# Sequence 0 of an attention-pack kernel with a channel mix: k and v loaded in runs of six tokens, p in one transfer, a planner without lag on one engine, and two tiles at a time in block 1's gates

## The chip, the cores and the metric

One NeuronCore of a Trainium2 chip runs the whole program. The time is the device time of one execution in microseconds. An execution that was also profiled gives the trace; its span runs from its first to its last instruction.

## The reference

Eight sequences (B) of 576 tokens (S), 8 heads (H) of 64 (D). For each sequence and head, 32 packed queries p attend to k and v, and the 576 queries q attend to the 32 packed results. The heads' outputs stand side by side as x (576 tokens by 512), which goes through a channel mix.

```
def sm_attn(qq, kk, vv):
    s = scale * np.matmul(qq, kk.transpose(0, 1, 3, 2))
    a = np.exp(s - np.max(s, axis=-1, keepdims=True))
    return np.matmul(a / (np.sum(a, axis=-1, keepdims=True) + 1e-09), vv)
p_packed = sm_attn(p, k, v)
x = sm_attn(q, p_packed, p_packed)           # heads side by side
x_prev = x one token later, 0 first
xk, xr = mu_k * x + (1 - mu_k) * x_prev, mu_r * x + (1 - mu_r) * x_prev
k = np.maximum(xk @ w_k, 0.0)                # 512 x 1024
out = sigmoid(xr @ w_r) * (k * k @ w_v)      # 512 x 512, 1024 x 512
```

All is float32. w_k is 512 by 1024, w_v 1024 by 512 and w_r 512 by 512.

## The kernel before

**Two halves.** The attention goes sequence by sequence (b = 0 to 7), the channel mix block by block: nine blocks (i = 0 to 8) of 512 tokens, four tiles of 128 tokens each. The mix's matmuls work on pairs: every operand is split into a high and a low part in a reduced format, and three products (high by high, high by low, low by high) take the place of one float32 product. `gates(i)` computes xr by w_r (lines 985 to 987), `keys(i)` xk by w_k (941 to 943), `values(i)` the squares by w_v (1015 to 1017). Block i needs x of the tokens 512 i to 512 i + 511; so sequence 0 and most of block 0 come first, and sequence 1 feeds block 1.

**Weights.** `convert` loads a 128x512 piece of a weight (tile st), and makes its high and low part with two instructions on ACT (lines 288, 302) and four on DVE (290, 292, 294, 304). Four pieces of w_r, eight of w_k and eight of w_v are done this way, during the first sequence and block 0.

**Attention of sequence 0.** `loads(0)` issues the loads: k by pairs of heads (raw, two transfers a pair), p by quarters (pin), v by parity of the head (vt and vl), q as k. k and q are transposed on PE by `transposed_on_pe` (line 400), 96 tokens at a time, and copied by ACT (line 409 for k, 405 for q). p is transposed by DVE (line 429). `front` multiplies p by k (line 453) and starts `weights_of` for the two head parities: a maximum over the tokens (566), its negative (568), the exponential on ACT (572), five transposes on PE (619, 620) and two copies (626, 628). `front` then multiplies by v (495), divides by the sums (510), transposes (516) and copies the result for all heads (524). In sequence 0 the second attention goes by tokens: `by_token` (line 720) and `weights_by_token` (737 to 763: maximum, difference, exponential, sum, reciprocal, product on DVE and ACT; transposes at 757). `shared` multiplies the packed results by mu, and `first_mix` (810) makes xr and xk of block 0 from them, by windows of 256 tokens.

**Sequence 1** has the same loads and PE transposes, and then `back` for its second attention (lines 636 to 694). Its result is copied into xt (851), and `mix` and `split` make xr and xk for block 1 from it, a chunk c of 128 channels at a time (888, 890, 896, 916, 918). Sequences 2 to 7 are transposed by DVE and by a trip through DRAM (far, aTd; line 487 is their product with v).

**What sets the order.** The program is written by a planner, `Flow`, as the kernel is built. Every part is a generator that asks for an engine with an estimated time (`vec`, `act`, `pe`, or `load` for SP's queue), for a buffer (`take` and `give`), or waits for an event. `run` picks the part that could start first; among equals, the one of the lowest rank. So each engine's order is fixed when the kernel is built, and on the chip each engine works it off in order, waiting at semaphores. A result is taken to be there LAG = 0.22 us after its instruction's end, also when the next instruction of the same part is on the same engine. Where `after` is given, that time counts instead. In idle time before block 0's gates, PE's order is filled with small matmuls (spare, line 1111).

**Buffers.** xk has 4 and sq 8 (both 1024 elements a partition); k and q of sequence 0 lie in them first. vt has 2 (v), xt 4 (577 pairs), tmp 4, pt 1, m 4 banks of PSUM and pa 2 pairs of banks. `gates(0)` works on two tiles at a time (STEP = 2), c by c; all other blocks on one.

Of the kernel before, what the change touches and what calls it, by code (L numbers as in the profile page):

```python
# [16 lines left out]
class Flow:  # L17
# [13 lines left out]
    class Part:  # L31
        def __init__(self, gen, rank, t, n):
            self.gen, self.rank, self.t, self.n = gen, rank, t, n
            self.want = None

# [77 lines left out]
    def start(self, part):  # L113
        engine, us, after, table = part.want
        ready = part.t if after is None else after
        return max(self.free.get(engine, 0.0), ready), ready
# [23 lines left out]
    def run(self):  # L140
        while self.parts:
            part = min(self.parts, key=self.order)
            self.parts.remove(part)
            engine, us, after, table = part.want
            start, _ = self.start(part)
            if engine is None:
                part.t, part.want = start, None
                self.go(part)
                continue
            if table and table != self.table:  # L150
                start += self.TABLE
                self.table = table
            if engine == "tensor":
                us = self.at_clock(start, us)
            self.free[engine] = start + us
            part.t = start + us + self.LAG
            part.want = None
            self.go(part)
# [5 lines left out]
def attn_pack_channel_mix(ctx: ExitStack, tc: tile.TileContext, q, k, v, p, mu_k, mu_r, w_k, w_v, w_r, out):  # L164
# [152 lines left out]
    def loads(b):  # L317
        flow.spawn(packed(b), lrank(b) - (0.03 if b else 0.015))
        for src, tag in ((k, "kT"), (v, "vt"), (q, "qT")):
# [5 lines left out]
            for pr in range(NPR):  # L325

                space = ("xk" if tag == "kT" else "sq") if b == 0 else "raw"
                slot = yield from flow.take(space)
                if b < EARLY:
# [25 lines left out]
    def values_of(b, h):  # L355

        slot = yield from flow.take("vt")
# [24 lines left out]
    def transposed_on_pe(tag, b, pr, raw_space, raw_slot, raw):  # L382
# [9 lines left out]
        for hf in range(2):  # L392
# [6 lines left out]
            for c in range(3):  # L399
                nc.tensor.transpose(bank[:, c * T6:(c + 1) * T6], raw[:T6, 3 * hf + c], ident[:T6, :T6])  # L400
            if hf:
                flow.give(raw_space, raw_slot)
            if beside:
                yield act(HS)
                nc.scalar.copy(t[:, hf * HS:(hf + 1) * HS], bank[:, :HS])
# [8 lines left out]
    def packed(b):  # L414

        slot = yield from flow.take("pt")
        pin = sb.tile([P, NPR, 32], F32, name="pin", tag="pin")
# [23 lines left out]
    def front(b):  # L441
# [8 lines left out]
        for hf in range(2):  # L450
# [9 lines left out]
        flow.give("pt", pts.pop(b)[0])  # L460
# [9 lines left out]
        for h in range(2):  # L470
# [20 lines left out]
            for c in range(5):  # L491
# [8 lines left out]
            flow.give("vt", sv)  # L500
# [60 lines left out]
    def weights_of(b, h, slot, s1, sm):  # L561
# [55 lines left out]
        tp = banks(slot).rearrange("p a b -> p (a b)")  # L617
        for c in range(4):
# [347 lines left out]
    def gates(i):  # L966
        for t in range(0, NT, STEP if i == 0 else 1):
            tiles = range(t, t + (STEP if i == 0 else 1))
# [171 lines left out]
```

## Time and profile before

| | |
|---|---|
| median of 3 runs | 599.82 us (599.34 to 601.22) |
| the profiled execution, its time | 601.94 us |
| its span | 599.8 us |
| busy in the span: PE, DVE, ACT | 587.4, 366.9, 313.2 us |
| mean granted clock of PE | 0.988 |
| read from HBM, written | 43.00 MB, 12.98 MB |

A time in a timeline counts from the span's start. PE is TensorE's matmul row and PEld its weight loads; a busy PE includes the filling matmuls, and a float32 matmul stands as two instructions. SPq is the queue that issues loads and stores. A row of a timeline gives the start, the length, engine, line, operation, out<-in, form and count; behind it in brackets the idle time before and what ended it. The granted clock is the share of TensorE's full clock.

### The profile page before, as it was taken

To read this page: it belongs to the slowest core of one execution; us is meant where nothing else is said; L and a number is where in the kernel's file an instruction comes from. 1 tells how busy PE (TensorE), PEld (TensorE's weight loads), DVE (VectorE), ACT (ScalarE), POOL (GpSimd) and SP (SyncE) were. 2 spreads that over 40 slices of the span, in tenths; PEclk is the share of its full clock that TensorE was granted. 3 is DMA by queue.
4 is the path that set the end of the run, shared out by engine and by line. 5 is a ranking of instruction groups with operands and counts; after the bars stand their busy time and mean duration, and the time that the engine had idled before them with its cause. 6 is when DMAs were issued, how large, how long until landed. Compare 5 with 4: busy or idle time off the path is not lost.

```text
span 599.8 us, 10305 instructions
## 1 busy us (share of the span) xinstructions
PE 587.4 (98%) x3997; PEld 462.2 (77%) x3997; DVE 366.9 (61%) x711; ACT 313.2 (52%) x561; POOL 7.5 (1%) x33
## 2 busy tenths in 40 slices
PE   8899999899999999999999999999999999999997
PEld 7877777477777777786867777778788888888885
DVE  1499999855888769836981987177404812551321
ACT  3558882663584685354824585258524703631410
POOL 3000000000000000000000000000000000000000
PEclk9799999989999999999999999999999999999999
DMA  8975943862664761664646343200100010001001
GB/s 200 304 218 164 248 94 51 203 126 48 144 138 111 153 143 28 174 126 92 139 115 139 75 84 99 72 1 0 69 2 1 0 72 0 1 0 71 1 0 70
DMA packets 170159, 56.64 MB, mean 94 GB/s; under 512 B 146936, under 2 KB 161408, under 8 KB 170112
## 3 DMA queue, kind: packets, MB, share of 16 engines
q1 hardware_dynamic: 169792, 55.86, 38.0%
q8 instruction: 31, 0.51, 0.4%
q0 software_dynamic: 320, 0.14, 0.1%
q14 instruction: 16, 0.13, 0.1%
HBM read 43.00 MB, written 12.98 MB: 93 GB/s over the span
## 4 chain that ended last, share of the span: by engine, by line
PE 84%; DVE 6%; DMA 4%; SPq 3%; ACT 1%; issue 1%; DVEq 0%
PE pvo L1015 11%; PE pvo L1016 10%; PE pvo L1017 10%; PE ph L941 10%; PE ph L943 9%; PE ph L942 9%; PE pr L985 5%; PE pr L987 5%; PE pr L986 5%; SPq L211 3%; DMA raw<-in_q 2%; PE pa L487 2%; PE pa L691 1%; PE spare L1111 1%; PE pa L636 1%; DMA vt<-in_v 1%
## 5 line engine op out<-in xcount | busy, mean ns | idle before, releaser
L941 PE MATMUL ph<-xk,wk_h 128*128 128x512 f32 x288 | 114.9, 399 | 0.0
L1015 PE MATMUL pvo<-wv,sq 128*128 128x512 f32 x288 | 114.7, 398 | 0.0
L943 PE MATMUL ph<-xk,wk_l 128*128 128x512 f32 x288 | 112.3, 390 | 0.0
L1016 PE MATMUL pvo<-wv,sq 128*128 128x512 f32 x288 | 112.3, 390 | 0.0
L942 PE MATMUL ph<-xk,wk_h 128*128 128x512 f32 x288 | 112.3, 390 | 0.0
L1017 PE MATMUL pvo<-wv,sq 128*128 128x512 f32 x288 | 112.2, 389 | 0.0
L959 DVE CAST sq<-r 128x512 fp32r<-128x512 f32 x72 | 30.0, 418 | 104.7 <-ACT r L955 102.5
L952 ACT ACTIVATE r<-ph 128x512 f32<-128x512 f32 x72 | 43.0, 598 | 85.7 <-PE ph L943 84.6
L1015 PEld LDWEIGHTS pvo<-wv,sq 128*128 128x128 f32 x288 | 54.0, 188 | 16.8 <-issue 5.8
L941 PEld LDWEIGHTS ph<-xk,wk_h 128*128 128x128 f32 x288 | 54.0, 188 | 15.9 <-issue 4.5
L943 PEld LDWEIGHTS ph<-xk,wk_l 128*128 128x128 f32 x288 | 54.1, 188 | 11.9 <-DVE wk_l L304 0.5
L1017 PEld LDWEIGHTS pvo<-wv,sq 128*128 128x128 f32 x288 | 54.1, 188 | 11.4
L1016 PEld LDWEIGHTS pvo<-wv,sq 128*128 128x128 f32 x288 | 54.1, 188 | 10.4
L942 PEld LDWEIGHTS ph<-xk,wk_h 128*128 128x128 f32 x288 | 54.1, 188 | 10.3
L985 PE MATMUL pr<-wr_h,xr 128*128 128x512 f32 x144 | 58.7, 408 | 1.8 <-ACT xr L916 1.8
L987 PE MATMUL pr<-wr_h,xr 128*128 128x512 f32 x144 | 57.6, 400 | 0.9 <-DVE xr L918 0.9
L896 DVE SCALAR_TENSOR_TENSOR x<-xt,mus,x 128x448 f32<-128x448 f32 (+6 forms) x112 | 53.2, 512 | 7.5 <-ACT x L890 7.5
L986 PE MATMUL pr<-wr_l,xr 128*128 128x512 f32 x144 | 57.1, 396 | 0.0
L890 ACT ACTIVATE x<-xt,mus 128x448 f32<-128x448 f32 (+6 forms) x112 | 54.2, 528 | 1.4 <-DVE xr L918 1.3
L997 ACT ACTIVATE sig<-pr 128x512 f32<-128x512 f32 x36 | 21.3, 601 | 58.3 <-PE pr L987 46.0
L961 DVE TENSOR_TENSOR sq<-r,sq 128x512 fp32r<-128x512 f32 x72 | 49.2, 685 | 1.4
L1026 DVE TENSOR_TENSOR sig<-pvo,sig 128x512 f32<-128x512 f32 x36 | 23.8, 685 | 38.3 <-PE pvo L1017 38.2
(117 smaller groups left out, 705.4 us busy)
## 6 DMA issues: line engine op xcount, KB each, us to landing
out<-sig SPq DMA_DIRECT2D x36, 256.0 KB, 2.5
vt<-in_v SPq DMA_DIRECT2D x16, 512.0 KB, 4.8
raw<-in_k SPq DMA_DIRECT2D x96, 72.0 KB, 2.8
raw<-in_q SPq DMA_DIRECT2D x96, 72.0 KB, 2.8
st<-in_moe_w_k SPq DMA_DIRECT2D x8, 512.0 KB, 7.7
st<-in_moe_w_v SPq DMA_DIRECT2D x8, 512.0 KB, 4.1
far<-at SPq DMA_DIRECT2D x12, 288.0 KB, 2.5
aTd<-far SPq DMA_DIRECT2D x12, 256.0 KB, 3.0
```

The lines of the kernel that those rows point to most:

```text
L890: nc.scalar.mul(x32[:, o:o + n], xts[b, c][:, 1 + s:1 + s + n], mus[:, j, c:c + 1])
L896: nc.vector.scalar_tensor_tensor(x32[:, o:o + n], xts[b, c][:, s:s + n], mus[:, j + 1, c:c + 1], x32[:, o:o + n], op0=ALU.mult, op1=ALU.add,)
L941: nc.tensor.matmul(ph, wk_h[:, c, fs], xh, start=(c == 0), stop=False)
L942: nc.tensor.matmul(ph, wk_h[:, c, fs], xl, start=False, stop=False)
L943: nc.tensor.matmul(ph, wk_l[:, c, fs], xh, start=False, stop=(c == NC - 1))
L961: nc.vector.tensor_tensor(hl[:, 1, :], r, hl[:, 0, :].bitcast(F32), op=ALU.subtract)
L985: nc.tensor.matmul(pr, xh[:, ts_], wr_h[:, c, :], start=(c == 0), stop=False)
L986: nc.tensor.matmul(pr, xh[:, ts_], wr_l[:, c, :], start=False, stop=False)
L987: nc.tensor.matmul(pr, xl[:, ts_], wr_h[:, c, :], start=False, stop=(c == NC - 1))
L1015: nc.tensor.matmul(pv[t], sh, wvs[f][:, 0, :], start=(f == 0), stop=False)
L1016: nc.tensor.matmul(pv[t], sh, wvs[f][:, 1, :], start=False, stop=False)
L1017: nc.tensor.matmul(pv[t], sl, wvs[f][:, 0, :], start=False, stop=(f == NF - 1))
```

## The change

Five edits:

- k of sequence 0: one transfer for a pair of heads, each partition taking six tokens that follow one another (1536 bytes a run) in place of 256-byte runs. A transpose takes two tokens of one head (128 columns) in place of one token of two heads. Afterwards a half of the partitions holds the even tokens and the other half the odd ones, so `front` needs p on both halves.
- p of sequence 0: one transfer with 256-byte runs, doubled by ACT, transposed by two PE transposes and copied by ACT.
- v of sequence 0: four transfers with 1536-byte runs into xt buffers. The weights a are then transposed in six pieces of 96 tokens (three sixths from each half), copied at once into an sq buffer, and multiplied by v in six steps.
- The second half of every q transpose of sequence 0 is copied by DVE in place of ACT.
- The planner: the next instruction of a part on the same engine, with nothing between, counts as ready without the lag. And `gates(1)` goes by two tiles like `gates(0)`.

```
     def start(self, part):
         engine, us, after, table = part.want
         ready = part.t if after is None else after
+        if after is None and part.last == (engine, ready):
+            ready -= self.LAG
         return max(self.free.get(engine, 0.0), ready), ready
...
             part.t = start + us + self.LAG
+            part.last = engine, part.t
...
+                if b == 0 and tag == "kT":
+                    raw = tile_([P, 2, 6 * D], F32, space, slot, "raw")
+                    yield from load(
+                        raw[:T6], src[b, 2 * pr:2 * pr + 2].rearrange("h (p c) d -> p h (c d)", p=T6), 0.5, 0.76,
+                    )
+                    back_to_issue()
+                    flow.spawn(transposed_on_pe(tag, b, pr, space, slot, raw), rank(b) + TR[tag], flow.free["dma"] + LANDS)
+                    continue
...
     def values_of(b, h):
+        if b == 0:
+            slots = []
+            for j in range(2):
+                slots.append((yield from flow.take("xt")))
+                vt = tile_([P, 2, 6 * D], F32, "xt", slots[-1], "vt")
+                yield from load(
+                    vt[:T6], v[b, 4 * j + h:4 * j + h + 3:2].rearrange("h (p c) d -> p h (c d)", p=T6), 0.5, 0.76,
+                )
+                if not j:
+                    back_to_issue()
+                vts[b, h, j] = vt
+            vts[b, h] = slots, None, None
+            flow.set(("vt", b, h))
+            return
...
-                nc.tensor.transpose(bank[:, c * T6:(c + 1) * T6], raw[:T6, 3 * hf + c], ident[:T6, :T6])
+                pair = raw[:T6, hf, 2 * D * c:2 * D * (c + 1)] if b == 0 and tag == "kT" else raw[:T6, 3 * hf + c]
+                nc.tensor.transpose(bank[:, c * T6:(c + 1) * T6], pair, ident[:T6, :T6])
...
             if beside:
-                yield act(HS)
-                nc.scalar.copy(t[:, hf * HS:(hf + 1) * HS], bank[:, :HS])
+                out_ = t[:, hf * HS:(hf + 1) * HS]
+                if hf:
+                    yield vec(HS)
+                    nc.vector.tensor_copy(out_, bank[:, :HS])
+                else:
+                    yield act(HS)
+                    nc.scalar.copy(out_, bank[:, :HS])
...
     def packed(b):
         slot = yield from flow.take("pt")
+        if b == 0:
+            sr = yield from flow.take("tmp")
+            rows = tile_([P, 2, 2, D], F32, "tmp", sr, "rows")
+            yield from load(rows[:, :, 0, :], p[b].rearrange("(j h) n d -> (h n) j d", j=2), 0.45, 0.25)
+            yield act(P)
+            nc.scalar.copy(rows[:, :, 1, :], rows[:, :, 0, :])
+            sp = yield from flow.take("pa")
+            pT = banks(sp)
+            yield pe(0.26)
+            for j in range(2):
+                nc.tensor.transpose(pT[:, 0, j * P:(j + 1) * P], rows[:, j].rearrange("p x d -> p (x d)"), ident)
+            flow.give("tmp", sr)
+            so = yield from flow.take("tmp")
+            pt = tile_([P, H, NP], F32, "tmp", so, "pt")
+            yield act(2 * P)
+            nc.scalar.copy(pt, pT[:, 0, :2 * P].rearrange("p (h n) -> p h n", h=H))
...
+        if b == 0:                                    # front: scores of p and k
+            for h in range(2):
+                for pr in range(NPR):
+                    for x, own in enumerate(HALVES):
+                        nc.tensor.matmul(
+                            s1[h][32 * pr:32 * pr + 32, x, :HS], pts[b][1][own, 2 * pr + h, :],
+                            ts["kT", b, pr][1][own, h * HS:(h + 1) * HS],
+                            start=True, stop=True,
+                        )
...
+            for c in range(0 if b else 6):            # front: product with v
+                for pr in range(NPR):
+                    own = slice(32 * pr, 32 * pr + 32)
+                    nc.tensor.matmul(
+                        pv[own, h, :D], aT[:T6, c, own], vts[b, h, pr // 2][:T6, pr % 2, c * D:(c + 1) * D],
+                        start=(c == 0), stop=(c == 5),
+                    )
...
+        if b == 0:                                    # weights_of
+            for c in range(6):
+                o = HS * (c % 2) + T6 * (c // 2)
+                nc.tensor.transpose(tp[:T6, c * P:(c + 1) * P], a[:, o:o + T6], ident)
+            flow.give("a", sa)
+            sT = yield from flow.take("sq")
+            aT = tile_([P, 6, P], F32, "sq", sT, "aT")
+            yield act(6 * P)
+            nc.scalar.copy(aT[:T6], tp[:T6, :6 * P].rearrange("p (a b) -> p a b", b=P))
...
     def gates(i):
-        for t in range(0, NT, STEP if i == 0 else 1):
-            tiles = range(t, t + (STEP if i == 0 else 1))
+        step = STEP if i < 2 else 1
+        for t in range(0, NT, step):
+            tiles = range(t, t + step)
```

More of the change, by code (lines that the diff above doesn't have):

```diff
@@ L34, in __init__ @@
             self.want = None
+            self.last = None
     def __init__(self):
@@ L416, in packed @@
         slot = yield from flow.take("pt")
+        if b == 0:
[14 more added lines that the diff above has]
+            nc.scalar.copy(pt, pT[:, 0, :2 * P].rearrange("p (h n) -> p h n", h=H))
+            flow.give("pa", sp)
+            flow.give("pt", slot)
+            pts[b] = so, pt
+            flow.set(("pt", b))
+            return
         pin = sb.tile([P, NPR, 32], F32, name="pin", tag="pin")
@@ L449, in front @@
         s1 = [banks(slot) for slot in slots]
-        for hf in range(2):
+        if b == 0:
[7 more added lines that the diff above has]
+                        )
+        for hf in range(2 if b else 0):
             for pr in range(NPR):
@@ L459, in front @@
             flow.give("kq", ts.pop(("kT", b, pr))[0])
-        flow.give("pt", pts.pop(b)[0])
+        flow.give("pt" if b else "tmp", pts.pop(b)[0])
         sm = const.tile([P, 2], F32, name="sm", tag=f"sm{b % 2}")
@@ L490, in front @@
                 continue
-            for c in range(5):
+            for c in range(0 if b else 6):
[5 more added lines that the diff above has]
+                    )
+            for c in range(5 if b else 0):
                 n = P if c < 4 else S - NQ
@@ L499, in front @@
             flow.give(*sT)
-            flow.give("vt", sv)
+            if b:
+                flow.give("vt", sv)
+            else:
+                for x in sv:
+                    flow.give("xt", x)
         summed = flow.t
@@ L617, in weights_of @@
         tp = banks(slot).rearrange("p a b -> p (a b)")
+        if b == 0:
[7 more added lines that the diff above has]
+            nc.scalar.copy(aT[:T6], tp[:T6, :6 * P].rearrange("p (a b) -> p a b", b=P))
+            flow.give("pa", slot)
+            aTs[b, h] = ("sq", sT), aT
+            flow.set(("aT", b, h))
+            return
         for c in range(4):
```

## The prediction, made before the changed kernel had run

> **What bounds the kernel now.** I read the page first, then the busy time by stretches, then the engines' timelines of the first 40 us, then the place where the chain of waits leaves TensorE after that.
>
> ```profile
> span 599.8 us, 10305 instructions
> PE 587.4 (98%) x3997; PEld 462.2 (77%) x3997; DVE 366.9 (61%) x711; ACT 313.2 (52%) x561; POOL 7.5 (1%) x33
> ...
> 23.90:27.90 4.00, 4.00 (x29) 4.00 (x28) 2.84 (x5) 2.77 (x6) 0.00 (x0) 0.73 1.02 382
> 27.90:60.00 32.10, 32.08 (x347) 24.57 (x347) 31.38 (x69) 21.61 (x48) 1.26 (x5) 1.00 0.65 206
> 60.00:83.00 23.00, 22.99 (x150) 17.89 (x148) 22.69 (x45) 19.68 (x35) 0.00 (x0) 1.00 0.70 190
> 83.00:112.00 29.00, 28.87 (x262) 21.14 (x261) 24.04 (x46) 13.28 (x27) 0.00 (x0) 1.00 0.50 100
> 125.10:599.00 473.90, 469.23 (x2932) 370.83 (x2931) 269.20 (x515) 233.66 (x399) 1.02 (x10) 1.00 0.31 72
> ```
>
> The columns are stretch, length, then busy us (instructions) of PE, PEld, DVE, ACT, POOL, then granted clock, DMA share, GB/s. After 125 us PE has no room: 469.23 of 473.90 at full clock, DVE at 57%. No edit there can win much. From 27.9 to 83 us PE and DVE are both full (DVE 31.38 of 32.1, 22.69 of 23.0): DVE there converts the weights just in time, so the start of the mix moves forward only as far as DVE's first work does. Before 24 us neither does useful work all the time; that part waits for loads:
>
> ```profile
> 0.73 4.66 SPq L211 DMA_DIRECT2D raw<-in_k  x8
> 5.44 1.94 SPq L211 DMA_DIRECT2D pin<-in_p  x4
> ...
> 9.96 8.00 SPq L211 DMA_DIRECT2D raw<-in_q  x8
> 18.00 2.15 SPq L211 DMA_DIRECT2D st<-in_moe_w_r  x4
> ```
> ```profile
> L211 SPq DMA_DIRECT2D raw<-in_k x2: 508/714/920, 3.9 to 4.5; - x2
> ...
> DMA to landing us min/median/max: 3.7/3.7/3.7
> ```
> ```profile
> L211 SPq DMA_DIRECT2D raw<-in_q x2: 505/506/507, 16.9 to 17.4; - x2
> ...
> DMA to landing us min/median/max: 2.7/3.4/4.1
> ```
> ```profile
> L211 SPq DMA_DIRECT2D st<-in_moe_w_r x4: 430/468/654, 18.0 to 19.5; - x4
> ...
> DMA to landing us min/median/max: 4.8/5.5/7.1
> ```
> ```profile
> 15.83 0.58 ACT L626 COPY aT<-pa 128x512 f32<-128x512 f32 x1
> ```
> ```profile
> 10.46 1.20 PE L453 MATMUL pa<-kT,pt 64*32 64x288 f32 x32
> 17.33 0.44 PE L400 MATMUL pq<-ident,raw 96*128 96x96 f32 x3 [1.53 <-DMA raw<-in_q]
> 25.87 4.39 PE L720 MATMUL s2t<-ppB,qT 128*128 128x64 f32 x40
> 38.23 0.47 PE L985 MATMUL pr<-wr_h,xr 128*128 128x512 f32 x1
> ```
> ```profile
> 23.96 0.43 DVE L290 TENSOR_SCALAR m<-m 128x512 uint32<-128x512 uint32 x1 [2.30 <-ACT m L288]
> 24.42 0.69 DVE L292 SCALAR_TENSOR_TENSOR m<-st,m 128x512 uint32<-128x512 uint32 x1
> 25.15 0.69 DVE L294 SCALAR_TENSOR_TENSOR m<-st,m 128x512 uint32<-128x512 uint32 x1
> 25.76 0.42 DVE L290 TENSOR_SCALAR m<-m 128x512 uint32<-128x512 uint32 x1
> ...
> 27.91 0.69 DVE L737 TENSOR_REDUCE m2t<-s2t 128x16 f32<-128x512 f32 x1 [1.00 <-PE s2t L720]
> ```
>
> The blocks are: SP's issues (start, length, name, count); the landing of k's last two issues, q's last two and w_r's four (start to landing); then rows of ACT, PE and DVE in time. Four v issues stand between p's and q's. k's last lands at 4.5 + 3.7 = 8.2, the last q at 17.4 + 4.1 = 21.5, the first w_r at 18.0 + 4.8 = 22.8, and DVE's steady work begins at 23.96. PE waited 1.53 us for q at 17.33. The first useful mix matmul is at 38.23. One further place loses PE time, block 1's gates:
>
> ```profile
> 19.25:26.05 6.80, 6.80 (x65) 6.47 (x53) 3.39 (x9) 4.23 (x12) 0.00 (x0) 0.50 1.00 342
> 114.00:118.00 4.00, 2.20 (x6) 0.97 (x6) 4.00 (x8) 3.84 (x10) 0.00 (x0) 1.00 0.88 272
> 114.17:122.27 8.10, 5.81 (x12) 2.77 (x13) 8.10 (x15) 6.91 (x17) 0.10 (x1) 0.75 0.79 192
> 118.25:125.05 6.80, 6.35 (x13) 3.95 (x14) 6.80 (x13) 5.48 (x10) 0.10 (x1) 0.50 0.68 109
> ```
> ```profile
> 52.21 0.39 PE L985 MATMUL pr<-wr_h,xr 128*128 128x512 f32 x1
> 52.44 0.39 PE L986 MATMUL pr<-wr_l,xr 128*128 128x512 f32 x1
> ```
>
> A gate matmul costs 52.44 − 52.21 = 0.23 us; tile 0's 12 took 8.10 us instead of 2.7, because DVE and ACT make xr chunk by chunk (both full in that row), and the clock was at 0.50 from 118.25 to 125.05.
>
> **The change, part by part.**
>
> *Loads.* The rate by packet size:
>
> ```profile
> DMA packets 4424, 1.16 MB, mean 232 GB/s; under 512 B 4317, under 2 KB 4424, under 8 KB 4424
> DMA packets 223, 0.23 MB, mean 326 GB/s; under 512 B 0, under 2 KB 223, under 8 KB 223
> DMA packets 761, 2.79 MB, mean 399 GB/s; under 512 B 82, under 2 KB 82, under 8 KB 760
> 16.30:17.40 1.10, 0.07 (x1) 0.10 (x2) 0.00 (x0) 0.12 (x1) 0.00 (x0) 1.00 0.09 18
> ```
>
> They are k (2 to 7 us, 256-byte runs), v (9.2 to 9.9, 1024-byte runs) and weights (24 to 31, 4096-byte runs). k and v now come in 1536-byte runs, which no row shows: between 326 and 399, I take 360 as 1536 is nearer 1024. k, v and q hold 8 x 576 x 64 x 4 bytes = 1.18 MB each: 3.3 us each where k took 5.1. p is 0.07 MB, 0.3 us; the POOL queue's mu rows (0.13 MB) about 0.6. From the first packet at 2.0 that is 2.0 + 6.6 + 0.3 + 0.6 = 9.5. q keeps its 256-byte runs: 1.18 MB at 232 = 5.1, so its packets end at 14.6. k's last landing, 8.2, was 0.8 after 2.0 + 5.1 and the mu rows' part up to then (7.4); so q's is at 15.4: 6.1 earlier than 21.5. SP does not hinder: 9 issues at some 0.55 (k's 8 took 4.66) put q's first issue at 5.7, not 9.96. Bounds: at 399 GB/s 6.7 earlier; if the hole of 16.30 to 17.40 (DMA share 0.09, cause not shown) comes again, 1.2 more, 4.9. I take 5.5, between the last two. w_r, which follows q on SP's queue, moves by as much, and so do w_k and block 1's loads behind it. The vt buffers stand unused by sequence 0, but v of sequence 1 is issued behind its k, so it gains nothing from that.
>
> *k and p.* Transposes of k stay 24 with a 0.64 us ACT copy a pair. p loses four issues and a 0.31 us DVE transpose; it gains on ACT two copies (0.26 and 0.40 by the nearest rows, 64x128 and 128x288) and two transposes on PE (0.25). They lie in line after p's landing, and on the same ACT as the last kT copy: 7.0 (2.0 + 3.3 + 0.6 + 0.3 + 0.8) + 0.3 + 0.3 + 0.6 + 0.4 = 8.6 for the first scores, 1.9 earlier than 10.46.
>
> *a and the first PV.* Six transposes for five, one copy of 768 for 512 + 128 (+0.1 us), 48 PE passes a head for 40 (below):
>
> ```profile
> 90.10 0.83 PE pa L495 x40
> ```
>
> That row of the chain makes it +0.2 a head: +0.5 in all on a chain that ran 6.2 us from 10.46 to its last aT copy (15.83 + 0.58, and 0.3 for the small copy: 16.7). So aT stands at 15.0, pm about 16.8, ppB 17.7. Its cover is q: with q at 16.0 and four of the eight qT copies moved from ACT to the idle DVE (0.4 each), the token scores (25.87) can start near 18. That is 7.9 earlier, more than w_r's 5.5, so DVE's start is what counts: 24.0 − 5.5 = 18.5. The half clock of 19.25 to 26.05 came after PE's 1.53 us wait; it costs nothing in the new sum as DVE sets the pace.
>
> *Order without lag on one engine.* An instruction of the same part that follows on the same engine is now put right behind, where the planner used to slip another part's in. L292 to L294, which depend on each other, start 0.73 apart; L294 to the next, free L290 0.61. So a dependent neighbour costs 0.12. Up to 83 us about 12 such pairs in the token softmax, 2 at nmx and 8 at the squares are at stake; some stood together already: 22 × 0.12 = 2.6 at most, below nothing if earlier results fill DVE's idle 1.16 us of 23.9 to 27.9 (4.00 − 2.84). I take +0.5.
>
> A page speaks against this term: the Trainium skill, "VectorE: DVE Perf Modes", section "The DRAIN you can't avoid", has every DVE instruction wait for the pipe, chained or not. By that rule the pairs would be free and the sum 0.5 us better; the 0.73 against 0.61 disagrees.
>
> First stage: −5.5 + 0.5 = −5.0, between −6.7 − 1.2 = −7.9 and −4.9 + 2.6 = −2.3. PE from 38.23 and DVE move together, as the w_k conversions start with their landing and DVE's queue.
>
> *Gates of block 1 by two tiles.* While chunk c + 1 of xr is made, PE now does c for two tiles: tile 1's 12 matmuls (2.7 us) fall into the 5.4 us of waiting. Idle from 114 to 118 goes from 1.8 us to about 0.6. If the clock then stays, the matmuls between 122.27 and 125.05 are saved 1.4 us; I take half, 0.7. So −3.4, from 0 (a second `m` bank late, or xr later by the new order) to −4.1. The second bank is one that values(0) frees when its product is taken:
>
> ```profile
> 111.20 1.38 DVE L1026 TENSOR_TENSOR sig<-pvo,sig 128x512 f32<-128x512 f32 x2 [0.87 <-PE pvo L1017]
> ```
>
> These are its second and third product, the second done near 111.9, before the first xr at 114. Behind the waiting PE stand only tiles 2 and 3, keys(1) and sequence 2's front, which wait as long today. What is late next is still the last xr chunk, and then the table load and sigmoids of tiles 0 and 1 on ACT, which lie beside tiles 2 and 3; their banks are needed by keys(1) only behind those.
>
> Sum: −5.0 − 3.4 = −8.4. The profiled execution took 601.94 us, 2.1 around its span and above the median; on it the sum gives 593.5, on the median of 599.82 it gives 591.4.
>
> **Rivals.**
> 1. DVE eats the early start: dependent pairs at 2.6 and the hole in the DMA again, −2.3, with the gates −3.4: 594.1; if half of the first stage's rest is lost too, 595.5. For it: DVE is full to 83. Against: 24.04 of 29.0 from 83 to 112 gives 5 us back.
> 2. The gates gain nothing, since xr bounds the block whatever the order: 599.8 − 5.0 = 594.8. For it: DVE and ACT full in 114.17 to 122.27. Against: 36 matmuls followed the last chunk, and 24 now do.
> 3. More: both upper bounds, −7.9 − 4.1: 587.8.
> 4. No change of the end: what starts early waits at 83 to 112 for sequence 1's softmax: 599.8. Against: that softmax hangs on the same loads.
> 5. Slower: the new order puts a front of sequences 2 to 7 too early in PE's queue, which is in order, as now happens once:
>
> ```profile
> 273.24 0.65 PE L487 MATMUL pa<-vt,aTd 128*32 128x64 f32 x32 [0.83 <-DMA aTd<-far]
> ```
>
> Once costs about 1.1 with its neighbour. At 1.4 us for each of six sequences the 8.4 us are gone; at 2.0 it ends at 603.4.
> 6. The clock falls again while the token scores run. A rule for it: the Trainium skill, "TensorE: Matmul & The Clock Gate", Part 4, says transposes do not count as busy, and the same page's Part 1 asks for an idle window of some 3.4 us. The trace dropped it at 118.25 after 1.8 us of idle in 4. The price by rows: token scores take 4.39; at half clock 4.4 more, of which DVE's w_r work hides half, 2.2: 593.6.
>
> **How the numbers follow.** Forecast 591.4, own range 588 to 594, chance 0.43; rival 1 0.15, rival 2 0.13, rival 3 0.07, rival 4 0.07, rival 5 0.09, rival 6 0.06. Within 0.3% (598.0 to 601.6, what a measurement can tell) is rival 4; faster is the forecast and rivals 1, 2, 3 and 6, 0.84; slower is rival 5. The range: 0.05 below 586.5 and 0.14 above 598.5.
>
> **What would show it.** q's last landing at 15 to 17; L453 near 8.6, L720 near 18, DVE's first L290 near 18.5; L985 first near 33; block 1's gates with under 1 us of idle and no half clock near 113 to 120. Wrong if k's or v's packets run under 326 GB/s, if DVE idles between 19 and 78, or if PE waits after 125 more than the 4.7 us of now.

## The result, and the profile after

| | median of 20 runs, us | lowest to highest |
|---|---|---|
| before | 599.11 | 597.48 to 601.22 |
| after | 602.42 | 599.70 to 608.64 |

Ratio 1.0073 (95%: 1.0052 to 1.0094): slower, by 3.3 us in the medians and 4.4 by the ratio, where 8.4 us less were forecast. The executions of kernels with the new loads spread, with the granted clock between 1.00 and 0.985, so the lowest and highest stand beside medians below. The profiled execution of after took 600.53 us, at full clock. That of before (601.94, clock 0.988) was one of its longest: it holds two stretches of 6.8 us at half clock, at 19.25 and at 118.25 us, while the 27 executions of before beside runs 1 to 4 stand at 0.990 to 0.997, most at 0.993 or 0.994, which is one such stretch (6.8 × 0.5 of 598).

The page of after, span and busy times:

```profile
span 598.3 us, 10325 instructions
...
PE 580.6 (97%) x3999; PEld 457.2 (76%) x3999; DVE 376.2 (63%) x714; ACT 313.3 (52%) x557; POOL 7.6 (1%) x33
```

DVE works 9.3 us longer than before (366.9) with three instructions more. Next after's stretches (columns as in the prediction), then its first matmul of each stage on PE, then three rows of DVE, its first conversion and the second and fourth low part of w_r:

```profile
27.90:60.00 32.10, 29.56 (x324) 22.30 (x324) 31.18 (x68) 21.29 (x49) 0.10 (x1) 1.00 0.62 180
...
115.80:126.50 10.70, 10.70 (x49) 8.85 (x48) 8.66 (x16) 7.22 (x11) 0.00 (x0) 1.00 0.77 194
126.70:598.00 471.30, 463.65 (x2903) 365.64 (x2901) 272.70 (x510) 230.64 (x393) 1.02 (x10) 1.00 0.31 71
```
```profile
9.81 1.20 PE L511 MATMUL pa<-kT,pt 64*32 64x288 f32 x32
...
21.04 4.29 PE L811 MATMUL s2t<-ppB,qT 128*128 128x64 f32 x40
...
34.79 0.47 PE L1078 MATMUL pr<-wr_h,xr 128*128 128x512 f32 x1
...
54.29 0.43 PE L1032 MATMUL ph<-xk,wk_h 128*128 128x512 f32 x1
```
```profile
22.08 0.42 DVE L294 TENSOR_SCALAR m<-m 128x512 uint32<-128x512 uint32 x1
...
35.80 0.68 DVE L308 TENSOR_TENSOR wr_l<-m,wr_h 128x512 fp32r<-128x512 f32 x1
...
44.83 0.68 DVE L308 TENSOR_TENSOR wr_l<-m,wr_h 128x512 fp32r<-128x512 f32 x1
```

The lines have new numbers: L294 to L308 are the conversions, L511 the scores of p, L811 the token scores, L1078 the gates, L1032 the keys, L782 (before: L691) the product of a and pm. The last column is the kernel of the sixth experiment, the changed kernel with one number altered. The column "run 3" is before with two tiles in block 1's gates alone: up to block 0's keys its engines run the same order as in before, and this trace ran at full clock, without the half clock at 19.25.

| us from the span's start | before | run 3 | forecast | after | lag 0.12 |
|---|---|---|---|---|---|
| first scores of p | 10.46 | 11.29 | 8.6 | 9.81 | 10.57 |
| token scores | 25.87 | 22.25 | 18 | 21.04 | 21.76 |
| DVE's first conversion | 23.96 | 22.39 | 18.5 | 22.08 | 20.79 |
| first gate matmul | 38.23 | 35.55 | 33 | 34.79 | 35.23 |
| first keys of block 0 | 53.57 | 50.88 | | 54.29 | 50.74 |
| first keys of block 1 | 131.77 | 125.42 | | 126.70 | 123.28 |
| last matmul | 595.45 | 589.88 | | 594.07 | 585.65 |

Against the profiled before, the first gate matmul is 3.4 us earlier, and at the keys of block 0 all of it is gone. Against run 3, which has no such half clock, the gate is only 0.8 earlier and the keys are 3.4 late. The low parts of w_r, which the gates need, come at 35.80 and 44.83; in run 3 the same two came earlier:

```profile
29.44 0.68 DVE L304 TENSOR_TENSOR wr_l<-m,wr_h 128x512 fp32r<-128x512 f32 x1
...
38.97 0.69 DVE L304 TENSOR_TENSOR wr_l<-m,wr_h 128x512 fp32r<-128x512 f32 x1
```
```profile
50.88 0.39 PE L941 MATMUL ph<-xk,wk_h 128*128 128x512 f32 x1
```

Block 1's gates run without a gap (10.70 of 10.70 us busy at full clock). Behind them PE is idle for 7.65 us of 471.3, where it was 4.67 of 473.9. After's longest waits of PE name the new one (columns: total, times, longest), and the last column shows what it waits for:

```profile
PE pa L782 <- DVE a L774: 5.4, 6, 1.4
PE tpt L848 <- DVE et L842: 2.5, 3, 1.4
```
```profile
96.29 0.74 DVE L764 TENSOR_REDUCE z<-e 128x18 f32<-128x576 f32 x1
97.07 0.18 DVE L766 TENSOR_SCALAR z<-z 128x18 f32<-128x18 f32 x1
97.28 0.27 DVE L768 RECIPROCAL z<-z 128x18 f32<-128x18 f32 x1
97.58 0.76 DVE L770 TENSOR_TENSOR e<-e,z 128x576 f32<-128x576 f32 x1
98.44 0.78 DVE L774 STREAM_TRANSPOSE a<-e 128x576 f32<-128x576 f32 x1
```
```profile
99.37 0.75 PE L782 MATMUL pa<-a,pm 32*64 32x288 f32 x16 [1.44 <-DVE a L774]
```

Five dependent instructions stand in a row. They start 0.78, 0.21, 0.30 and 0.86 apart; the planner reckons 0.67, 0.09, 0.18 and 0.67 (its `vec`: 0.07 + 1.04 ns an element). It took the transpose to be done about half a microsecond too soon, and so put the product too early into PE's queue, which is in order.

### The profile page after: what moved, and what is told of

It is laid out like the page before. It is cut to its first block, busy times and chain, and to the rows that moved or that the text cites. A ratio compares the mean times of both kernels' runs of the same rounds, so it can differ in the third digit from the quotient of the medians.

```text
span 598.3 us, 10325 instructions
## 1 busy us (share of the span) xinstructions
PE 580.6 (97%) x3999; PEld 457.2 (76%) x3999; DVE 376.2 (63%) x714; ACT 313.3 (52%) x557; POOL 7.6 (1%) x33
## 4 chain that ended last, share of the span: by engine, by line
PE 73%; DVE 16%; DMA 6%; ACT 2%; issue 2%; SPq 1%; DVEq 0%; ACTq 0%
PE pvo L1108 9%; PE pvo L1109 9%; PE pvo L1110 9%; PE ph L1032 8%; PE ph L1034 8%; PE ph L1033 8%; PE pr L1078 5%; PE pr L1079 5%; PE pr L1080 5%; DVE sq L1052 2%; PE pa L553 2%; PE pa L782 1%; DVE m L296 1%; DMA raw<-in_q 1%; DMA pin<-in_p 1%
## 5 line engine op out<-in xcount | busy, mean ns | idle before, releaser
L1032 PE MATMUL ph<-xk,wk_h 128*128 128x512 f32 x288 | 115.3, 400 | 0.0
L1032 PEld LDWEIGHTS ph<-xk,wk_h 128*128 128x128 f32 x288 | 54.0, 188 | 17.2 <-issue 5.9
L1078 PE MATMUL pr<-wr_h,xr 128*128 128x512 f32 x144 | 57.2, 397 | 0.0
L1080 PE MATMUL pr<-wr_h,xr 128*128 128x512 f32 x144 | 56.1, 390 | 0.0
```

The lines of the kernel that those rows point to most:

```text
L1032: nc.tensor.matmul(ph, wk_h[:, c, fs], xh, start=(c == 0), stop=False)
L1078: nc.tensor.matmul(pr, xh[:, ts_], wr_h[:, c, :], start=(c == 0), stop=False)
L1080: nc.tensor.matmul(pr, xl[:, ts_], wr_h[:, c, :], start=False, stop=(c == NC - 1))
```

## Experiments

### The parts one by one

Run numbers are the order of the runs. Theory: the order without lag is the loser, as its product of a and pm stands too early. Rival: the loads. Edits: the two planner lines taken out of after (1), the same lines alone put into before (2), `step = STEP if i < 2 else 1` alone put into before (3), and after without both (4).

```
 e1 and e4, against after:
-        if after is None and part.last == (engine, ready):
-            ready -= self.LAG
 e4, too:
-        step = STEP if i < 2 else 1
+        step = STEP if i < 1 else 1
```

> The changed kernel with the planner's lag of 0.22 us back on one engine; loads, p and the two-tile gates stay. Theory (the order without lag puts the product of a2 and pm, L691 of the kernel before, some 1 us too early into PE's queue, PE then waits for DVE's transpose of a, and its clock falls in some executions): these waits of 0.8 to 1.4 us go, the executions agree within 2 us, and the time is 592 to 596. Rival (the new loads delay the w_r conversions and so keys(0), which starts at 54.29 and not at 53.57): still 598 or more, waits or not.

> The kernel before with the order without lag alone. Theory: waits of some 1 us at the product of a2 and pm in most of sequences 1 to 7, 6 to 8 us in all, and lower clocks in some executions: 603 to 608. Rival (loads are to blame): within 1 us of the kernel before, 598 to 600.

> The kernel before with block 1's gates by two tiles alone. By the prediction's step: 3.4 us less (595.7), half clock at 118 us gone. Theory: the same, as this part is not what failed. Rival (xr bounds the block, the wait only moves): within 1 us of the kernel before.

> The kernel before with sequence 0's new k, v, p and q copies alone, lag and one-tile gates as before. By the prediction's first stage less its lag term: 5.5 us less (593.6). Theory: 2 to 4 less, as w_r's first landing in the changed kernel was 19.98 against 22.82, 2.8 earlier. Rival (the loads delay the conversions): no gain, 599 or more, with keys(0) at 53.5 or later.

| | loads | tiles | lag | median, us | ratio to before |
|---|---|---|---|---|---|
| 1 | new | 2 | 0.22 | 598.01 (595.13 to 606.25) | 0.9995 (0.9973 to 1.0017) |
| 2 | old | 1 | none | 599.42 (598.87 to 600.61) | 1.0013 (1.0004 to 1.0023) |
| 3 | old | 2 | 0.22 | 597.04 (596.38 to 599.04) | 0.9981 (0.9970 to 0.9991) |
| 4 | new | 1 | 0.22 | 601.47 (599.58 to 602.67) | 1.0047 (1.0030 to 1.0064) |

The theory held in part: taking the lag edit out of after wins 4.4 us, but 598.01 is not the 592 to 596 that it expected, and alone the edit costs before only 0.8, where 603 to 608 was expected. The loads (run 4 has all the edits on k, v, p and q), from which 5.5 us were hoped, lose 2.8 by themselves.

That the edit costs so little alone is not because it does no harm there. In run 2 PE waits 5.2 us for the same a, and block 0's keys start at 55.39. But block 1's gates, with one tile at a time, take 10.9 us at full clock, where before's took 17.6 (114.17 to 131.77), partly at half clock:

```profile
PE pa L695 <- DVE a L687: 5.2, 7, 1.0
```
```profile
115.30:126.20 10.90, 10.90 (x50) 9.01 (x49) 8.01 (x15) 7.37 (x11) 0.00 (x0) 1.00 0.78 176
```

So in an order without lag these gates run full with one tile too, and after's 10.70 is no proof of the two tiles; no run has the new loads without lag and with one tile. In 1 and 4 PE stands in the second product with v for a reason that is no data; this is run 1:

```profile
18.73 0.86 PE L558 MATMUL pa<-vt,aT 96*32 96x64 f32 x43
22.45 0.31 PE L558 MATMUL pa<-vt,aT 96*32 96x64 f32 x5 [2.85 <-issue]
```

### How much lag

```
-            ready -= self.LAG
+            ready -= self.LAG - 0.12
```

This makes an instruction ready 0.12 us after the one before it (the text below says 0.10; it ran with 0.12). Two more ran with 0.06 and 0.17, and two with 0.12 in some parts only:

```
+            ready -= self.LAG - (0.12 if part.gen.__name__ == "back" else 0.0)     # e13
+            ready -= self.LAG - (0.0 if part.gen.__name__ == "back" else 0.12)     # e14
```

> The changed kernel with a lag of 0.10 us in place of none for the next instruction of a part on the same engine (dependent neighbours on DVE measured 0.10 to 0.12 longer than free ones). Theory: the order without lag is too early by some 0.1 us an instruction, which put the product of a and p ahead of its transpose six times for 5.4 us; with 0.10 these waits should be under 1 us in all, and the median 3 to 4 us under the changed kernel's 602.4: 598 to 599.5. Rival: the waits only stand for idle time that other waits would take: they go, others come, the time stays at 601 to 603.

> The changed kernel with a lag of 0.06 us. Theory: what counts is how far the lag lies under the 0.10 to 0.12 us that a dependent neighbour takes longer on DVE: 0.06 leaves half of it, waits for the transpose a of 2 to 3.5 us in all (5.4 without lag, none with 0.12), 595 to 599. Rival: the 592.2 was one lucky order among many, and any other lag gives 597 to 602 with waits elsewhere.

> The changed kernel with a lag of 0.17 us, halfway from 0.12 to the 0.22 that the planner had (598.0 there). Theory: no operand comes late, so no waits for a; a little idle time is planned for each dependent pair: 592.5 to 595.5. Rival of a lucky order: 597 to 600. Rival: the lag of 0.22 was bad because of one late instruction fetch, not of its length: then this has either that stall and 597 to 598, or none and 592 to 594.

> The changed kernel with a lag of 0.12 us for same-engine successors in the part back only (the second attention of sequences 1 to 7, which ends in the product of a and p), none in all other parts. The changed kernel is at 602.4, and at 592.2 with 0.12 in all parts; open is which instructions lose the 10 us. Theory P (the product stands too early on TensorE, 5.4 us of waits for a, and the clock falls after some of them): most of it is won here, 594 to 597.5. Theory F (the token softmax's order on DVE in the first stage holds up the conversion of w_r, 3.5 to 5 us there): little is won, 598.5 to 601, block 0's keys still start near 54.3.

> The other half: no lag in the part back, 0.12 us in all other parts. Theory P: the waits for a stay at 4 to 5.5 us, 597 to 600.5. Theory F: block 0's keys start near 50.7 as with 0.12 everywhere, and 593 to 596.5. If both hold in part, this and the other run lie at 595 to 599 each, and their gains add up to about 10.

| lag, us | median, us | ratio to before |
|---|---|---|
| none | 602.42 (599.70 to 608.64) | 1.0073 (1.0052 to 1.0094) |
| 0.06 | 595.09 (594.32 to 605.28) | 0.9945 (0.9929 to 0.9962) |
| 0.12 | 592.16 (591.72 to 597.78) | 0.9910 (0.9881 to 0.9938) |
| 0.17 | 597.56 (595.75 to 600.96) | 0.9986 (0.9969 to 1.0003) |
| 0.22 | 598.01 (595.13 to 606.25) | 0.9995 (0.9973 to 1.0017) |
| 0.12 in back alone | 604.66 (598.43 to 606.27) | 1.0096 (1.0061 to 1.0131) |
| 0.12 in all but back | 595.20 (593.46 to 601.89) | 0.9950 (0.9928 to 0.9973) |

Ten microseconds lie between none and 0.12, where 3 to 4 were expected. Medians here mix executions with and without the standstill of TensorE that is told of below. Among those at a clock of 0.999 or more the medians are 600.65 (none, 8 executions), 594.87 (0.06, 8), 592.03 (0.12, 4), 596.52 (0.17, 5) and 596.19 (0.22, 6). The page of the kernel with 0.12, its longest wait at the product, its DVE beside the token softmax, and its first keys:

```profile
span 589.9 us, 10293 instructions
...
PE 579.5 (98%) x3989; PEld 456.2 (77%) x3989; DVE 367.9 (62%) x714; ACT 305.3 (52%) x553; POOL 7.6 (1%) x33
```
```profile
PE pa L782 <- DVE z L768: 0.3, 1, 0.3
```
```profile
25.30 0.68 DVE L828 TENSOR_REDUCE m2t<-s2t 128x16 f32<-128x512 f32 x1
25.90 0.68 DVE L298 SCALAR_TENSOR_TENSOR m<-st,m 128x512 uint32<-128x512 uint32 x1
26.50 0.68 DVE L830 TENSOR_TENSOR et<-s2t,m2t 128x512 f32<-128x512 f32 x1
27.10 0.68 DVE L828 TENSOR_REDUCE m2t<-s2t 128x16 f32<-128x512 f32 x1
27.70 0.68 DVE L308 TENSOR_TENSOR wr_l<-m,wr_h 128x512 fp32r<-128x512 f32 x1
...
39.20 0.69 DVE L308 TENSOR_TENSOR wr_l<-m,wr_h 128x512 fp32r<-128x512 f32 x1 [0.27 <-ACT wr_h L306]
```
```profile
50.74 0.39 PE L1032 MATMUL ph<-xk,wk_h 128*128 128x512 f32 x1
```

The same 714 DVE instructions take 367.9 us in place of 376.2; with lags of 0.06, 0.17 and 0.22 it is 367.2, 367.9 and 368.2. In these rows, with lag, the softmax and the conversions alternate, and each starts 0.60 after the one before; without lag each runs in a row of its own, where dependent neighbours start 0.72 apart. Only the order differs. Counted in the traces, 512 of DVE's instructions start before the one in front has ended with 0.12, and 424 without lag. So the second low part of w_r is there at 27.70 in place of 35.80, the last at 39.20 in place of 44.83, and block 0's keys start 3.55 us sooner.

The two partial kernels split the rest. In back alone, 598.43 at best, the product's waits go, but not the late w_r (block 0's keys at 54.39); its median, 604.66, lies outside what either theory expected. In all but back, 593.46 at best, 1.8 us of waits for a are left; its trace is an execution with the standstill and a half clock behind it, so it does not show w_r's times. Against 599.70 and 591.72 at best that is 1.3 and 6.2 of 8.0: the larger part was the order outside back, not the waits at the product, which the theory had put first. How much of the 6.2 lies in the first stage is shown only by the 3.55 us at block 0's keys. In DVE's busy time the halves are even, 3.6 and 3.7 of the 8.3 us (back alone, then all but back):

```profile
PE 582.5 (98%) x3999; PEld 457.4 (77%) x3999; DVE 372.6 (62%) x714; ACT 313.4 (53%) x557; POOL 7.6 (1%) x33
```
```profile
PE 587.2 (98%) x3989; PEld 464.3 (77%) x3989; DVE 372.5 (62%) x714; ACT 310.0 (52%) x557; POOL 7.6 (1%) x33
```

The runs with 0.06 and 0.17 were a miss in what they were to show. At 0.06 no wait for a was left, where 2 to 3.5 us were expected: not the length of the lag but its being there makes DVE alternate. The run with 0.17 missed its 592.5 to 595.5. They are slower than 0.12, 0.17 by the stall told of below and both by other waits, PE for xr in the gates, as in these rows (0.06, then 0.17):

```profile
PE pr L1080 <- DVE xr L1009: 1.8, 3, 1.1
```
```profile
PE pr L1080 <- DVE xr L1009: 3.0, 5, 1.1
```

With 0.12 they are 0.5 in all. So some 3 us of its advantage over its neighbours lie in one order among several, and no run shows that 0.12 is more than a good draw there.

### Loads and tiles under that lag

Run 9 is before with the planner lines at 0.12; run 10 has the two tiles besides; run 15 is the kernel with 0.12 and `i < 1` in `gates`.

> The kernel before with one edit: a lag of 0.12 us in place of 0.22 for the next instruction of a part on the same engine. Open is which part of the change gave the 592.2 that the changed kernel reaches with such a lag. Theory A: the loads and the two tiles are worth the 8 us that the prediction gave them, once the order is not too early: then this kernel, with neither, is at 597.5 to 599. Theory B: the loads are worth nothing on the time, the shorter but not too short lag itself is the gain: 592.5 to 595.

> The kernel before with a lag of 0.12 us and with block 1's gates by two tiles, the old loads. Theory A (loads worth some 5 us): 595 to 597.5, three to five over 592.2. Theory B (loads worth nothing): 591 to 593.5. Both: gates of block 1 in one piece of 12 to 13.8 us with no half clock.

> The changed kernel with a lag of 0.12 us in all parts and block 1's gates by one tile again. It completes the table of loads by tiles at this lag: 600.7 with neither, 595.8 with two tiles, 592.2 with both. Theory: the two tiles are worth about as much with the new loads as without (4.9): 595.5 to 598, waits for xr of 3 us or more in block 1's gates and a half clock there. Rival: with the earlier loads xr is ready in time by itself: 592 to 594.

| lag 0.12 | one tile | two tiles |
|---|---|---|
| old loads | 600.70 (600.36 to 601.41) | 595.84 (594.56 to 596.18) |
| new loads | 597.80 (595.34 to 603.32) | 592.16 (591.72 to 597.78) |

Ratios to before: 1.0034 (1.0021 to 1.0047) and 0.9948 (0.9936 to 0.9960); 0.9990 (0.9967 to 1.0013) and 0.9910 (0.9881 to 0.9938). Here both edits win, as the prediction said: the tiles 4.9 and 5.6 us, more than its 3.4, the loads 2.9 and 3.7 (2.6 and 2.3 by the ratios), less than its 5.5. Neither of the two theories held whole: the lag alone gains nothing (600.70), and the loads are not worth 5. In the stretch of block 1's gates of runs 9 and 10:

```profile
112.50:130.70 18.20, 14.75 (x50) 10.15 (x49) 14.53 (x26) 12.64 (x23) 0.10 (x1) 0.81 0.62 130
```
```profile
112.00:126.10 14.10, 12.04 (x49) 8.46 (x49) 13.28 (x24) 8.70 (x18) 0.10 (x1) 1.00 0.62 140
```

Four microseconds less, 2.7 of them busy time at a half clock that is gone; this pair, and not after's trace, shows the mechanism of the two tiles. In run 15 PE waited 2.3 us for xr there, less than the 3 expected, and its profiled execution had no half clock.

### The rate of the loads

> Only loads, two of each kind of 576 to 1024 KB, one kind after the other on one queue, and a store at the end; none of the attention or the mix is computed. Kinds by partitions and bytes in a run: 96 of 1536, 128 of 1024, 96 of 1024, 128 of 1536, 512, 768, 2048, 4096. Theory: the run length sets the rate, and 1536 bytes are slower than 1024: in the changed kernel's 2 to 8 us they moved at 285 GB/s, where the prediction took 360; here 280 to 300 GB/s for both 1536 kinds, 350 to 400 for 1024 on 128 partitions. Rival: the mu rows and other small packets beside them slowed them: then 1536 alone reaches 360 to 400. Rival: 96 partitions in place of 128 do it: then both kinds of 96 are alike and slower than both of 128.

It computes neither attention nor mix. The prediction took 360 GB/s for runs of 1536 bytes. After's first row from 2 to 8 us, then this kernel's windows: 96 partitions of 1536 bytes (1.7 to 5.5), 128 of 1024 (7.5 to 11; before 7.1 packets of the kind in front run beside them), 96 of 1024 (13.5 to 16), 128 of 1536 (18.6 to 20.4), 128 of 512 (21 to 25).

```profile
DMA packets 1483, 1.68 MB, mean 279 GB/s; under 512 B 414, under 2 KB 1483, under 8 KB 1483
```
```profile
DMA packets 641, 0.96 MB, mean 253 GB/s; under 512 B 16, under 2 KB 641, under 8 KB 641
...
DMA packets 1197, 1.21 MB, mean 345 GB/s; under 512 B 18, under 2 KB 1197, under 8 KB 1197
...
DMA packets 592, 0.61 MB, mean 243 GB/s; under 512 B 16, under 2 KB 592, under 8 KB 592
...
DMA packets 456, 0.67 MB, mean 370 GB/s; under 512 B 11, under 2 KB 456, under 8 KB 456
...
DMA packets 2309, 1.17 MB, mean 293 GB/s; under 512 B 19, under 2 KB 2309, under 8 KB 2309
```

The last rival is right: 1536 bytes run at 370 GB/s on 128 partitions and at 253 on 96; 1024 at 345 and 243. The longer run wins little where the partitions are 96. So the change helped the rate of k, which had 256-byte runs on 96 partitions (232 GB/s), and lowered that of v, which had 1024-byte runs on 128 (326). The Trainium skill, "SBUF — State Buffer", section "Door 1: The DMA port swizzle", has partitions 0 to 63 share one half of the DMA ports and 64 to 127 the other half; an estimate from that page is 3/4 of the full rate for 96, as 64 of them fall on one half. The measured 0.68 and 0.70 lie a little under it.

### The stall of TensorE, and the longer executions

The trace has a queue of its own for instructions. In before its first packet within the span runs at 14.72 us, and PE does not wait. In six traces PE has a wait that is put down to issue in a product of sequence 0 with v, each time right behind the 449th instruction of PE and PEld together:

| run | packet starts, us | PE stands, us | PE goes on after the packet's start | half clock then, us |
|---|---|---|---|---|
| 1 | 20.03 | 19.59 to 22.45 | 2.42 | 3.4 |
| 4 | 20.34 | 20.19 to 22.71 | 2.37 | 3.4 |
| 12 | 20.94 | 20.81 to 23.40 | 2.46 | 3.4 |
| 14 | 19.62 | 19.84 to 21.97 | 2.35 | 17.1 |
| 15 | 17.87 | 19.50 to 20.24 | 2.37 | none |
| 18 | 17.85 | 19.70 to 20.81 | 2.96 | none |

In 18 the packet itself took 1.68 us, in the others 0.88 to 0.94. The two traces of after have the same standstill in small: the packets start at 16.64 and 16.32, and the instruction behind the 449th at 19.13 and 18.67, 2.49 and 2.35 later, and 0.34 and 0.61 us behind the start of the one in front, where 0.08 is usual there. So the wait is for this packet. Windows of half a microsecond, from 14.5 in before and from 19.5 in run 14:

```profile
q8 instruction: 1, 0.02, 13.9%
```
```profile
q8 instruction: 1, 0.02, 11.7%
```

SP now issues w_r from 14.4 us in place of 18.0 (13.7 to 15.8 in the traces of this section, 16.8 in run 3), so its 512 KB transfers are in the queues when the packet is asked for. When that is shows only from the earliest packets: in runs 2, 3, 5, 9 and 10 they run when PE has started 222 to 232 instructions. PE reaches its 225th at 13.3 us in before, and at 14.7 to 16.8 in the kernels with the new loads and no early packet. Run 14's profiled execution, 601.89 us where its lowest is 593.46, shows what follows:

```profile
18.98 0.86 PE L560 MATMUL pa<-vt,aT 96*32 96x64 f32 x43
21.97 0.43 PE L560 MATMUL pa<-vt,aT 96*32 96x64 f32 x5 [2.12 <-issue]
```
```profile
21.50:38.60 17.10, 16.63 (x85) 16.23 (x85) 12.11 (x28) 5.10 (x10) 1.17 (x4) 0.50 0.54 193
```

A wait of 2.12 us, and 17.1 us at half clock behind it. To move the packet ahead of w_r, filling matmuls were replaced by more and smaller ones, so that PE passes its 225th instruction sooner: in run 1's kernel (5), in after (7) and in the kernel with 0.12 (17); 18 is the latter without it, on the same chip, and 16 is after once more.

```
+    small = [5]                    # e17: [14], and range(2)
     def fill():
+        if small[0]:
+            small[0] -= 1
+            for _ in range(6):
+                nc.tensor.matmul(spare[:32, :64], ident[:, :32], ident[:, :64], start=True, stop=True)
+            return
         nc.tensor.matmul(spare[:, :P], ident, ident, start=True, stop=True)
```

> Base: the changed kernel with the planner's lag back (598.01 us). Edit: the first five filling matmuls are replaced by six small ones each, some 100 more TensorE instructions before 5 us, nothing else. In that base TensorE stood 2.85 us in the second product with v at 19.4, put down to issue, while one 16384-byte packet of the instruction queue ran at 20.03; before the change that packet ran at 14.7. Theory: the fetch of TensorE's next instructions is asked for when it has passed some 225 of them, and now finds 512 KB transfers of w_r ahead of it in the DMA queues. It should then run near 11 to 12.5 with this edit, the 2.85 us and the half clock at 22.6 go, the token scores move from 26.33 to 22 to 23.5, block 0's gates from 38.7 to 35 to 36.5, and the median is 594.5 to 596, with most executions within 1.5 us. Rival: the stall is no fetch (a hole in the records, or a wait for data): it stays, at another instruction, and the time stays at 597 to 599. Rival: the stall goes, but DVE sets the pace there: scores earlier, gates(0) still at 38, time 597 to 598.5.

> The changed kernel with the same 100 small TensorE instructions early, nothing else. Theory: most executions of the changed kernel (602 to 608) have the late instruction fetch and a half clock behind it, which its profiled one (600.5) did not have; with the early fetch all executions should be like that one or better, median 599 to 600.5. Rival: the longer executions come from the waits of the product of a and p and the clock drops behind those; then the median stays at 601.5 to 603.

> The changed kernel as it is, on the same chip as the three others. Theory: 600 to 603; a longer execution than 600.5 shows, if it is the profiled one, a half clock behind one of the six waits for a or a stall of 2.5 us by a late instruction fetch near 19.5 us, which the shown one did not have. Rival: the longer executions come from loads that land late; then its profile has the same waits and clock and a later first stage.

> The changed kernel with a lag of 0.12 us, and each of the first 14 filling matmuls replaced by two small ones of about the same time together, so that TensorE passes its 225th instruction some 56 instructions sooner. Theory: the longer executions of these kernels (to 597.8 with this lag) are those in which the instruction packet comes late, behind w_r's transfers, and TensorE then stands 2 us and the clock falls; with the packet asked for before w_r is issued they go: all executions at 591.5 to 593, clock 0.998 or more, no wait put down to issue, the packet at 13 to 15.5. Rival: they come from the waits for data in the first stage and stay: some executions of 594 to 602 at a lower clock.

> The changed kernel with a lag of 0.12 us once more, on the same chip as the run beside it: 592 to 595 in the median, with longer executions at a lower clock among them (one of six at 597.8 and one at 594.6 before).

| | without | lowest clock | with early packet | lowest clock |
|---|---|---|---|---|
| 1 and 5 (lag 0.22) | 598.01 (595.13 to 606.25) | 0.985 | 598.00 (596.07 to 602.45) | 0.997 |
| after, 16 and 7 | 602.42 (599.70 to 608.64); 606.44 (600.39 to 610.08) | 0.985 | 600.92 (600.43 to 601.66) | 0.998 |
| 18 and 17 (lag 0.12) | 593.59 (591.16 to 600.03) | 0.986 | 593.22 (592.49 to 593.85) | 1.000 |

There are 12, 5 and 4 executions with the early packet, and 6 of run 18. Ratios to before: 5 0.9987 (0.9969 to 1.0004), 7 1.0037 (1.0025 to 1.0049), 16 1.0092 (1.0058 to 1.0125), 17 0.9908 (0.9889 to 0.9927), 18 0.9904 (0.9874 to 0.9933). The packet runs at 13.41, 13.03 and 13.41, no wait is put down to issue, and in 7 and 17 the long executions are gone (11 of after's 20 took more than 602 us, none of the 5 of run 7 did; with so few in 17 and 18 that pair shows little by itself). In 5 the longest fell from 606.25 to 602.45, and its trace still has 3.4 us of half clock, at 182 us. The best executions got no shorter: the small matmuls cost time of their own (in run 5 the first 30 took 6.20 us, and the scores of p started at 13.2 for 10.1), so run 5 missed its 594.5 to 596, run 7 its 600.5 by 0.4, and run 16 its 603. Why the packet is late in one execution and in time in the next is open. The long executions of after itself were not caught in a trace (both of its traces are at full clock), so that they are this is drawn from runs 14 and 7, and from the clock: 17.1 us at half clock are 0.014 of the span, and after's two longest, 608.34 and 608.64, stand at 0.985.

## Why the prediction was wrong, point by point

By the ratios to before, with the old lag of 0.22, the three parts come to this, one put on the other: two tiles −1.1 us (run 3), the loads on top +0.8 (run 1), no lag on top +4.7 (after); each is sure to some 2 us. The prediction had −3.4, −5.5 and +0.5. Two steps failed, the loads by 6.3 us and the order by 4.2; the other way round (loads first, run 4, then tiles, run 1) the loads are off by 8.3 and the tiles by 0.3.

- **The loads**, −5.5: the token scores came 4.8 us earlier than in the profiled before, not 7.9, and DVE's first conversion 1.9, not 5.5; against run 3 it is 1.2 and 0.3. k and v ran at 279 GB/s, not 360. The two neighbouring rows that bounded the rate were on 128 partitions, k and v are now on 96. Under the old lag the loads won nothing (runs 1 and 4): w_r's early issue now stands in front of PE's instruction packet, a term that the sum did not have. Where the packet is in time, run 5, block 0's keys still start at 51.61, after run 3's 50.88, though its small matmuls cost time there. Only with a lag of 0.12 do the loads win 2 to 4 us: keys at 50.74 with the new ones and 52.86 with the old (run 10).
- **The order without lag**, +0.5, at most 2.6: it cost 4.4 us against the old lag (after against run 1) and 10 against a lag of 0.12. The pitch, 0.73 against 0.61, was right and is what DVE's 8.3 us are made of. The count, 22 pairs up to 83 us, was about right too: of the 80 overlaps that are lost against run 1 (504 to 424), 18 lie before 83 us. Left out were the other 62 and, above all, what hangs on the order: w_r's conversions behind the token softmax, and PE's in-order queue. Rival 5 had the latter, and nearly the time (603.4), but with a front of a later sequence and its DMA; it was the second attention's product and its DVE transpose, six times, 0.38 to 1.44 us. That its time came near is luck.
- **The half clock at 19.25**, said to cost nothing: the profiled execution of before was 2.8 us over the median of 20. In run 3, whose first stage is as in before and had none, SP issued w_r at 16.8, not 18.0, the token scores started at 22.25, not 25.87, DVE's first conversion at 22.39, not 23.96, and block 0's keys at 50.88, not 53.57. So 1.6 to 3.6 of the time to be won were in that execution alone.
- **The gates**, −3.4: right in mechanism where there is a lag (runs 9 and 10), but the idle time did not fall under 1 us there: 2.06 of 14.10 are left. Alone under the old lag they win 1.1 by the ratio of run 3; with 0.12 4.9 and 5.6. What they are worth without lag was not run, and run 2 says that it may be nothing.
- **The signs it named** went off: k and v under 326 GB/s, and PE waits after 125 us at 7.65 in place of 4.67. First scores 9.81 for 8.6, token scores 21.04 for 18. q's last landing, 13.8 + 2.9 = 16.7, kept to its 15 to 17.
- **The sum** itself, 591.4, is about what the kernel with a lag of 0.12 gives (592.16 and 593.59). That is luck, with loads smaller and tiles larger than forecast: against run 3 its keys of block 0 are only 0.14 us earlier, where the prediction put 5.0 of its 8.4.

## What to carry to other kernels

A planner's lag of zero says that a dependent instruction may stand right behind its producer; on a full engine it pays to let another stream slip in between, so keep a small lag, and look at an engine's busy time for the same count of instructions. An edit that costs nothing alone may cost much beside another, when both take away the same wait (runs 2 and 3 both remove the half clock of block 1's gates): test it on top of the others. Loads that are issued earlier also stand earlier in front of everything else in the queues, the engines' own instructions among them. Before forecasting from one profiled execution, see how its clock and time stand to the others, or its accidents are counted as gains.

## What the runs showed of the hardware

- Dependent neighbours on DVE start 0.72 us apart, independent ones 0.60, at 0.68 us of length (128x512), which sums to 8.3 us of busy time (376.2 against 367.9, 714 instructions each). The Trainium skill, "VectorE: DVE Perf Modes", section "The DRAIN you can't avoid", has the next instruction wait until the pipe is empty, chained or not, and adds that one that is not held starts earlier. The prediction told only the first half; the 0.60 agrees with the addition.
- TensorE's instruction packet (16384 bytes) can come late behind data: 0.3 us (after) to 2.85 us (run 1) of standstill behind the 449th instruction, ended 2.35 to 2.49 us after the packet's start where the packet took 0.88 to 1.36 us; after the four longest 3.4 to 17.1 us of half clock. The Trainium skill, "Runtime: NRT & Kernel Launch", section "Instruction fetch mechanics", has such refills come over a DMA queue of the sequencer's own and calls the cost mostly hidden; here it was wholly hidden in before, and not in the six traces above, all with w_r's 512 KB transfers issued earlier than in before.
- Loads to 96 partitions ran at 243 to 253 GB/s, the same runs to 128 at 345 to 370 (run 8).
